# Another order of instructions for chunks 2 to 5 of an attention and feed-forward kernel

## The chip, the cores and the metric

The kernel runs on one core of one Trainium2 chip, in one launch. The metric is the device time of one execution in microseconds (us), the median over runs.

## What is computed

The first part is masked attention over 8 batches of 8 heads, 576 positions, 64 numbers a head. The first four heads of a batch look at the last 32 positions (local), the other four at every 32nd position before (strided). The second part is a feed-forward layer on the 4608 rows of 512 numbers that the heads give together, all in 32-bit floats:

```python
scores = scale * np.matmul(q, k.transpose(0, 1, 3, 2))
mask_local = (rel >= 0) & (rel < stride)
mask_strided = (rel >= 0) & (pos[None, :] % stride == pos[:, None] % stride)
...
attn = attn / (np.sum(attn, axis=-1, keepdims=True) + 1e-09)
x = np.ascontiguousarray(attn_out.transpose(0, 2, 1, 3)).reshape(B, S, H * D)
...
xn = (x - mu) / np.sqrt(var + 1e-06) * g_ln
ch = np.maximum(xn @ w_ch1, 0.0) @ w_ch2
return (x + ch).astype(np.float32)
```

w_ch1 is 512 x 2048, w_ch2 is 2048 x 512.

## The kernel before

**Chunks.** The 4608 rows are cut into nine chunks of 512 rows. Chunks 0 to 7 are the first 512 rows of each batch, chunk 8 the 64 rows left of each. A matrix product in full precision is three matmuls of TensorE: every operand is held as a high part (ScalarE rounds it) and a low part (the rest, by DVE or GpSimd), and high x high, high x low and low x high are added up in PSUM, where TensorE writes.

**Chunks 2 to 5** stand in `pair(c, p)` (L1317), with p from 0 to 7 for each chunk c, 32 calls. One call computes two of the 16 blocks of 128 columns of the first layer for all 512 rows, as a 2 x 2 block product by seven products in place of eight (Winograd's form). A product (`product2`, L1290, matmuls at L1299) is six matmuls 128 x 256. The weights' whole blocks a11, a12, a22 lie in SBUF, the four sums s1 to s4 of blocks are computed once in chunk 1 (`w_sums`, L802 on), kept in DRAM (`sd`) and brought back as needed: `stage_w(n)` (L1231) is a transfer sw<-sd issued by SyncE (SP), `split_w(n)` (L1236) makes high parts on ScalarE (L1240) and low parts on GpSimd (L1241). A call uses block n (s2 and one more sum) and n+1.

Products go to PSUM areas: x1 = a11 b11 with a12 b21 added later, x2 = s2 t2 with s3 t3 added, x3 = s1 t1 with s4 b22 added, x4 = a22 t4. Sums of these give four quarters: ScalarE copies x1 to p1 (L1331), DVE adds (`add2`, L1304) into u2, u3 and p1, and `quarter` (L1306) takes the relu's high part on ScalarE (L1309) and its low part on DVE (L1310). Each quarter puts two groups in a queue. A group (`group`, L889, matmuls at L902) is three matmuls 128 x 512 that add to an area po of the second layer; `run_groups(k)` issues k of the queue between products. After the last of 16 groups of an area `finish` (L874) takes it out (L876, DVE) and stores it (L879). Two areas po share one tile of two PSUM banks. Other areas: ps_h and ps_b one bank each, ps_m two.

**Attention beside it.** Heads are worked on in 32 twos (`Pair`s) that the generator `pieces` (L1071) hands out step by step, one `next(gen)` after each product. One step, `m_piece` (L687), is the block on TensorE: scores of the next two heads and outputs of these two (L452, L521), into ps_m (`m`) and the bank `n`. Behind it stand on DVE the mask (L480), the row maximum (L493) and the division of the outputs (`v_divide`, L571), on GpSimd the subtraction (L498), on ScalarE the exponential (L504). Others store the outputs (`v_store`, L584 to L589, SP), load them back in another shape (`x_raw`, L600, four transfers by ScalarE) and transpose them (`x_blocks`, L615, DVE), transpose q and k (`t_piece`, L427, DVE), load q and k (`load_qk`, L363, eight transfers by SP), v (`load_v`, L401 to L408) and x for the closing (`x_load`, L732 and L734). `half_c` (L1213) hands out the steps of statistics and x loads.

**What sets the order.** Each engine runs its instructions strictly in the order of the code, and the semaphores between them follow from the tiles. Transfers of SP and ScalarE are issued in those engines' order too. The x loads, the staged blocks and other input tiles share one pool of seven buffers. In `pair` the areas ps_h and ps_b change roles when a block has used one. Chunk 0 is set by a table; chunks 1 and 6 (`plain`, L1244) run the first layer in whole blocks of 512 columns, with attention beside; chunks 7 and 8 go through a loop with seven products of 512 columns (L1432) behind them.

## Time and profile before

| | us |
|---|---|
| median of the runs | 1019.4 (1016.4 and 1022.4) |
| the profiled execution, its own time | 1022.6 |
| its span | 1020.7 |
| TensorE (PE) busy | 906.2 (89%) |
| VectorE (DVE) busy | 567.0 (56%) |
| ScalarE (ACT) busy | 284.1 (28%) |
| GpSimd (POOL) busy | 350.9 (34%) |

Times in the trace count from the span's start. Matmuls are pipelined and their ends modelled, so the shares say how full an engine is, and not whether it is the limit. A wait is put down to the engine whose semaphore came last. PEclk is the mean clock that TensorE was granted as a share of full speed.

### The profile page before, as it was taken

To read this page: it belongs to the slowest core of one execution; us is meant where nothing else is said; L and a number is where in the kernel's file an instruction comes from. 1 tells how busy PE (TensorE), PEld (TensorE's weight loads), DVE (VectorE), ACT (ScalarE), POOL (GpSimd) and SP (SyncE) were. 2 spreads that over 40 slices of the span, in tenths; PEclk is the share of its full clock that TensorE was granted. 3 is DMA by queue.
4 is the path that set the end of the run, shared out by engine and by line. 5 is a ranking of instruction groups with operands and counts; after the bars stand their busy time and mean duration, and the time that the engine had idled before them with its cause. 6 is when DMAs were issued, how large, how long until landed. Compare 5 with 4: busy or idle time off the path is not lost. (4 is left out here: it accounts for less than half of the span.)

```text
span 1020.7 us, 20720 instructions
## 1 busy us (share of the span) xinstructions
PE 906.2 (89%) x7981; PEld 746.7 (73%) x7981; DVE 567.0 (56%) x1171; ACT 284.1 (28%) x590; POOL 350.9 (34%) x420
## 2 busy tenths in 40 slices
PE   7899989989688889889888888887879999999997
PEld 6688868777577767777677677666758787888776
DVE  5899943645655666565745565455345543333343
ACT  4786511111322232223222232222111122112121
POOL 5686725662424252324324252223100201112000
PEclk9999999999899999999899998999899999999999
DMA  9899646888576657756575576765566415332021
GB/s 191 220 261 295 145 94 152 199 205 185 148 165 139 128 132 194 155 132 135 152 164 125 119 161 172 152 151 128 120 183 116 95 42 186 103 104 72 8 76 42
DMA packets 382698, 146.64 MB, mean 144 GB/s; under 512 B 297732, under 2 KB 360072, under 8 KB 382600
## 3 DMA queue, kind: packets, MB, share of 16 engines
q1 hardware_dynamic: 305544, 131.23, 51.4%
q10 hardware_dynamic: 77056, 14.10, 7.8%
q8 instruction: 63, 1.03, 0.4%
q14 instruction: 35, 0.29, 0.1%
HBM read 104.56 MB, written 40.70 MB: 142 GB/s over the span
## 5 line engine op out<-in xcount | busy, mean ns | idle before, releaser
L902 PE MATMUL po<-w,hq 128*128 128x512 f32 x768 | 232.4, 417 | 22.9 <-ACT hq L1309 14.7
L902 PE MATMUL po<-w,hh 128*128 128x512 f32 x640 | 202.3, 398 | 7.4 <-DVE x L876 7.4
L902 PEld LDWEIGHTS po<-w,hq 128*128 128x128 f32 x768 | 136.0, 201 | 42.8 <-ACT hq L1309 16.5
L902 PEld LDWEIGHTS po<-w,hh 128*128 128x128 f32 x640 | 118.9, 190 | 35.2 <-DVE x L876 10.8
L902 PE MATMUL po<-w,hl 128*128 128x512 f32 x320 | 125.8, 393 | 0.0
L1299 PE MATMUL x<-xh_a,w 128*128 128x256 f32 x256 | 65.0, 314 | 32.0 <-ACT p L1331 25.6
L498 POOL TENSOR_TENSOR sm<-sm,mx 128x640 f32<-128x640 f32 (+1 forms) x31 | 39.4, 1270 | 143.9 <-DVE mx L493 128.7
L1299 PE MATMUL x<-xh_b,w 128*128 128x256 f32 x384 | 84.5, 283 | 1.9 <-DVE p L1304 1.8
L1299 PEld LDWEIGHTS x<-xh_a,w 128*128 128x128 f32 x256 | 48.7, 210 | 47.0 <-ACT p L1331 35.0
L870 DVE SCALAR_TENSOR_TENSOR hl<-ph,hh 128x512 fp32r<-128x512 f32 x48 | 32.9, 686 | 79.1 <-ACT hh L865 79.1
L1241 POOL TENSOR_TENSOR xh_a<-sw,xh_a 128x256 fp32r<-128x256 f32 x32 | 24.0, 749 | 149.4 <-ACT xh_a L1240 144.1
L744 POOL TENSOR_TENSOR rs<-rs,mhalf 128x1 f32<-128x1 f32 x36 | 20.4, 566 | 150.3 <-DVE rs L743 150.3
L1299 PEld LDWEIGHTS x<-xh_b,w 128*128 128x128 f32 x384 | 65.4, 188 | 8.0 <-DVE p L1304 2.6
L902 PEld LDWEIGHTS po<-w,hl 128*128 128x128 f32 x320 | 60.6, 189 | 13.0
L1241 POOL TENSOR_TENSOR w<-sw,w 128x256 fp32r<-128x256 f32 x64 | 47.2, 760 | 52.9 <-ACT w L1240 52.9
L865 ACT ACTIVATE hh<-ph 128x512 fp32r<-128x512 f32 x48 | 28.5, 595 | 131.1 <-PE ph L860 105.8
L1310 DVE SCALAR_TENSOR_TENSOR hq<-u,hq 128x256 fp32r<-128x256 f32 x64 | 30.8, 482 | 53.4 <-ACT hq L1309 53.4
L1304 DVE TENSOR_TENSOR u<-x,p 128x256 f32<-128x256 f32 x64 | 26.8, 419 | 53.9 <-ACT p L1331 36.0
L504 ACT ACTIVATE sm<-sm 128x648 f32<-128x648 f32 (+1 forms) x32 | 23.7, 741 | 109.9 <-POOL sm L498 105.0
L1299 PE MATMUL x<-xh_a 128*128 128x256 f32 x128 | 31.2, 306 | 26.1 <-DVE xo L571 13.3
L1299 PE MATMUL x<-xl_b,w 128*128 128x256 f32 x192 | 53.8, 280 | 0.0
L853 PE MATMUL ph<-xh,w 128*128 128x512 f32 x124 | 51.1, 412 | 2.5 <-DVE hl L870 2.5
(228 smaller groups left out, 1887.1 us busy)
## 6 DMA issues: line engine op xcount, KB each, us to landing
s<-in_moe_w_ch_dram SPq DMA_DIRECT2D x32, 512.0 KB
sw<-sd SPq DMA_DIRECT2D x64, 256.0 KB
out_dram<-x SPq DMA_DIRECT2D x32, 256.0 KB
raw<-in_q_dram SPq DMA_DIRECT2D x108, 72.0 KB
raw<-in_k_dram SPq DMA_DIRECT2D x108, 72.0 KB
wd<-w SPq DMA_DIRECT2D x24, 256.0 KB
ringa<-wd SPq DMA_DIRECT2D x24, 256.0 KB
xds<-xo SPq DMA_DIRECT2D x32, 162.0 KB
```

The costliest lines, as they stand in the source:

```text
L498: eng.tensor_tensor(out=sm, in0=sm, in1=mx[:, :, 0:nt].unsqueeze(3).broadcast_to([P, 2, nt, sm.shape[3]]), op=ALU.subtract)
L504: nc.scalar.activation(out=self.smv, in_=self.smv, func=AF.Exp, scale=SCALE)
L744: nc.gpsimd.tensor_tensor(out=rs, in0=rs, in1=mhalf, op=ALU.pow)
L853: nc.tensor.matmul(ph, w1h[:, cc], x[:, cc, :], start=(new and n == 0 and i == 0), stop=False)
L865: nc.scalar.activation(out=hh, in_=ph, func=AF.Relu)
L870: nc.vector.scalar_tensor_tensor(out=hl, in0=ph, scalar=0.0, in1=hh.bitcast(F32), op0=ALU.max, op1=ALU.subtract)
L902: nc.tensor.matmul(po[c, i], hx, w, start=(n_po[c, i] == 0 and n == 0), stop=(n_po[c, i] == NFC - 1 and n == 2))
L1241: nc.gpsimd.tensor_tensor(out=w[:, 1], in0=t[:, k], in1=w[:, 0].bitcast(F32), op=ALU.subtract)
L1299: nc.tensor.matmul(ps, wx, xx[:, j], start=(start and j == 0 and i == 0), stop=(j == 1 and i == 2), skip_group_check=not start)
L1304: nc.vector.tensor_tensor(out=out, in0=ps, in1=x, op=ALU.add)
L1310: nc.vector.scalar_tensor_tensor(out=hl, in0=src, scalar=0.0, in1=hh.bitcast(F32), op0=ALU.max, op1=ALU.subtract)
```

## The change

In `pair` the products come in the order a11, s2, s1, a12, s3, a22, s4 (before: a11, s2, a12, s3, s1, a22, s4), with four PSUM areas: x1 and later x4 in ps_h, x2 in ps_b, x3 in ps_m, which the attention block uses only at the start of an even pair. The block stands at a fixed place, ahead of the first product of each even p, and directly in front of it. The low parts of quarters (now a class `Quarter`) come one addition later, that of the last quarter in the next call; two groups run at the call's end. The exponential and its subtraction stand behind the copy of x1 and the split of block n+1; the split of n+2 stands ahead of the loads of x by ScalarE and of the relu q22. Loads and transposes of attention have fixed places. `finish` runs for the two areas of a po tile together. Around it: the sums in another order and on other engines, their store in three transfers, chunk 1 leaving seven groups instead of five, the last attention blocks in chunk 6, s1 before a12 in the loop of chunk 8.

The core of the diff (the function `pair` whole, then the small parts):

```diff
-    def quarter(c, f, i0, src):
-        t = hp_.tile([P, CH], F32R, tag=("hh", "hl")[i0 // 2], name=f"hq{c}_{f}_{i0}")
-        hh, hl = t[:, 0:HC], t[:, HC:CH]
-        nc.scalar.activation(out=hh, in_=src, func=AF.Relu)
-        nc.vector.scalar_tensor_tensor(
-            out=hl, in0=src, scalar=0.0, in1=hh.bitcast(F32), op0=ALU.max, op1=ALU.subtract)
-        add_groups(c, f, i0, (hh, hl))
-
-    def l1_bank(i, name):
-        return pools[i].tile([P, CH], F32, tag="h", name=name)[:, 0:HC]
+    class Quarter:
+
+        def __init__(self, c, f, i0, src):
+            self.key, self.src = (c, f, i0), src
+            t = hp_.tile([P, CH], F32R, tag=("hh", "hl")[i0 // 2], name=f"hq{c}_{f}_{i0}")
+            self.h = t[:, 0:HC], t[:, HC:CH]
+            nc.scalar.activation(out=self.h[0], in_=src, func=AF.Relu)
+
+        def low(self):
+            nc.vector.scalar_tensor_tensor(
+                out=self.h[1], in0=self.src, scalar=0.0, in1=self.h[0].bitcast(F32), op0=ALU.max,
+                op1=ALU.subtract)
+            add_groups(*self.key, self.h)
+
+    late = []
+
+    def late_low():
+        if late:
+            late.pop().low()
 
     def pair(c, p):
-        last = p == NFC // 2 - 1
+        even = p % 2 == 0
+        last, more = p == NFC // 2 - 1, c < wide - 2
         n = NFC * (c - 2) + 2 * p
-        end = NFC * (wide - 3) - 2
-        nv = visits[0]
-        third[0] = pools[1]
-        next(gen, None)
-        if visits[0] == nv:
-            pools.reverse()
-            third[0] = pools[1]
-        half_c(c, 2 * p)
-        run_groups(1)
-        x1 = l1_bank(0, f"x1_{c}_{p}")
+        fetch = n < NFC * (wide - 3) - 2
+        i = NHP * (c + 1) + p // 2
+        now, nxt = pairs[i], pairs[i + 1]
+        if even:
+            ps = bank(f"m{i}"), ps_b.tile([P, CH], F32, tag="h", name=f"n{i}")
+            parts = nxt.s_blocks(ps)
+            av = now.v_blocks(ps)
+            nxt.s_mask(parts)
+            late_low()
+            now.v_divide(av)
+            now.v_store()
+            nxt.s_max()
+        else:
+            late_low()
+        x1 = ps_h.tile([P, CH], F32, tag="h", name=f"x1_{c}_{p}")[:, 0:HC]
         product2(p, "a11", "b11", x1)
         nc.scalar.copy(out=p1_t, in_=x1)
-        next(gen, None)
         split_w(n + 1)
+        if even:
+            nxt.s_sub()
+            nxt.s_exp()
+        else:
+            nxt.p_load(nc.scalar)
         run_groups(1)
-        x2 = l1_bank(1, f"x2_{c}_{p}")
+        x2 = ps_b.tile([P, CH], F32, tag="h", name=f"x2_{c}_{p}")[:, 0:HC]
         product2(p, "s2", "t2", x2)
         add2(u2_t, x2, p1_t)
-        next(gen, None)
-        if last and c < wide - 2:
+        if even:
+            pairs[i + 2].load_v()
+        else:
+            now.x_blocks()
+        half_c(c, 2 * p)
+        if fetch:
+            stage_w(n + 2)
+        if last and more:
             x_split("b11")
         run_groups(1)
+        x3 = bank(f"x3_{c}_{p}")[:, 0:HC]
+        product2(p, "s1", "t1", x3)
+        if not even:
+            pairs[i + 2].t_piece()
+        run_groups(1)
         product2(p, "a12", "b21", x1, False)
-        quarter(c, 2 * p, 0, x1)
-        next(gen, None)
-        if last and c < wide - 2:
+        q = Quarter(c, 2 * p, 0, x1)
+        q.low()
+        if fetch:
+            split_w(n + 2)
+        if even:
+            nxt.p_turned()
+        if last and more:
             x_split("t2")
-        if n < end:
-            stage_w(n + 2)
+            x_split("t1")
         run_groups(1)
         product2(p, "s3", "t3", x2, False)
         add2(u3_t, x2, p1_t)
-        if last and c < wide - 2:
-            x_split("b21")
-        run_groups(1)
-        next(gen, None)
-        half_c(c, 2 * p + 1)
-        x3 = l1_bank(0, f"x3_{c}_{p}")
-        product2(p, "s1", "t1", x3)
         add2(p1_t, x3, u3_t)
-        quarter(c, 2 * p + 1, 2, p1_t)
-        next(gen, None)
-        if n < end:
-            split_w(n + 2)
+        if even:
+            now.x_raw(nc.scalar)
+        q22 = Quarter(c, 2 * p + 1, 2, p1_t)
+        if not even and i + 3 < NP:
+            pairs[i + 3].load_qk()
+        if fetch:
+            stage_w(n + 3)
         if last:
             late_x(c, 0)
         run_groups(1)
-        x4 = l1_bank(1, f"x4_{c}_{p}")
+        x4 = ps_h.tile([P, CH], F32, tag="h", name=f"x4_{c}_{p}")[:, 0:HC]
         product2(p, "a22", "t4", x4)
+        if even:
+            nxt.v_sums()
         add2(u3_t, x4, u3_t)
-        quarter(c, 2 * p + 1, 0, u3_t)
-        next(gen, None)
-        if n < end:
-            stage_w(n + 3)
+        q21 = Quarter(c, 2 * p + 1, 0, u3_t)
+        q22.low()
+        half_c(c, 2 * p + 1)
         if last:
             late_x(c, 1)
         run_groups(1)
         product2(p, "s4", "b22", x3, False)
         add2(u2_t, x3, u2_t)
-        quarter(c, 2 * p, 2, u2_t)
-        next(gen, None)
+        late.append(Quarter(c, 2 * p, 2, u2_t))
+        q21.low()
         if last:
             late_x(c, 2)
             late_x(c, 3)
         if p in (1, 7):
             w_whole(2 * (c - 2) + int(p > 1))
-        run_groups(1)
+        run_groups(2)
```

```diff
-        if n_po[c, i] == NFC:
+        if n_po[c, i] == NFC and i % 2:
+            finish(c, i - 1)
             finish(c, i)
...
-    LO = dict(b11=nc.vector, t2=nc.gpsimd, b21=nc.vector, t3=nc.gpsimd, t1=nc.vector, t4=nc.gpsimd,
-              b22=nc.vector)
+    LO = dict(b11=nc.vector, t2=nc.gpsimd, t1=nc.vector, b21=nc.gpsimd, t3=nc.vector, t4=nc.gpsimd,
+              b22=nc.gpsimd)
...
-    SUMS = ("s2", "s3", "s1", "s4")
+    SUMS = ("s2", "s1", "s3", "s4")
...
-            short = i < 3 * NHP - 1 or i in (25, 27, 29)
+            short = i < 3 * NHP - 1 or i >= NP - NHP
...
+        elif c < wide - 1:
+            at, late = (4, 5, 8, 9), 2
...
-    plain(1, NT - 1)
+    plain(1, 1)
...
+    late_low()
     run_groups(len(groups))
...
+    gen = pieces(NP - NHP, NP)
     plain(wide - 1, NT)
...
+        product(p, "s1", "t1", x3)
         product(p, "a12", "b21", x1, False)
         ha = h_pair(A, 2 * p, x1)
```

**Two places in the order of instructions.** The first is ScalarE in chunk 3, call p = 2. A row is line, operation, what is written, what is read and the shape; hq is a quarter's high part, sm the scores, p1 the copy of x1, w1_13, w1_15 the split block n+1 (in the place of a weight tile), xh_a and xl_a the split block n+2. Before:

```order
L1309 ACTIVATE hq3_2_2_4903<-u2_2145 128x256
L504 ACTIVATE sm0_191<-sm0_191 128x2x6x54
L1331 COPY p1_2144<-x1_3_2_4992 128x256
L1240 ACTIVATE w1_13_1844<-sw21_4891 128x256
L1240 ACTIVATE w1_15_2016<-sw21_4891 128x256
L1309 ACTIVATE hq3_4_0_5028<-x1_3_2_4992 128x256
L600 DMA xraw4_0_5046<-xdl_201 32x16x32 x4
L1309 ACTIVATE hq3_5_2_5067<-p1_2144 128x256
L1240 ACTIVATE xh_a_2142<-sw22_5031 128x256
L1240 ACTIVATE xl_a_2143<-sw22_5031 128x256
```

Now:

```order
L1314 ACTIVATE hq3_2_2_4901<-u2_2145 128x256
L1348 COPY p1_2144<-x1_3_2_4986 128x256
L1244 ACTIVATE w1_13_1844<-sw21_4875 128x256
L1244 ACTIVATE w1_15_2016<-sw21_4875 128x256
L504 ACTIVATE sm0_191<-sm0_191 128x2x6x54
L1314 ACTIVATE hq3_4_0_5039<-x1_3_2_4986 128x256
L1244 ACTIVATE xh_a_2142<-sw22_5018 128x256
L1244 ACTIVATE xl_a_2143<-sw22_5018 128x256
L600 DMA xraw4_0_5062<-xdl_201 32x16x32 x4
L1314 ACTIVATE hq3_5_2_5067<-p1_2144 128x256
```

The exponential (L504) has moved behind the copy and the split of n+1, and the split of n+2 (the last two L1240 rows) ahead of the loads of x and of the relu hq3_5_2.

The second place is DVE in the same call, from the start of the call; m and n are the outputs of the attention block in PSUM, den the rows' sums, xo the divided outputs, mx the row maximum. Before:

```order
L1310 SCALAR_TENSOR_TENSOR hq3_2_2_4903<-u2_2145,hq3_2_2_4903 128x256
L480 TENSOR_TENSOR sm0_191<-m4_0_4912,mask_s_137 128x2x5x54
L480 TENSOR_TENSOR sm0_191<-n4_0_4913,mask_s_137 64x54
L480 TENSOR_TENSOR sm0_191<-m4_0_4912,mask_s_137 64x54
L571 TENSOR_TENSOR xo_195<-n4_0_4913,den1_198 128x4x64
L571 TENSOR_TENSOR xo_195<-n4_0_4913,den1_198 64x64
L493 TENSOR_REDUCE mx4_3_4977<-sm0_191 128x12
L571 TENSOR_TENSOR xo_195<-m4_0_4912,den1_198 128x3x64
L571 TENSOR_TENSOR xo_195<-m4_0_4912,den1_198 128x64
L571 TENSOR_TENSOR xo_195<-m4_0_4912,den1_198 64x64
L1304 TENSOR_TENSOR u2_2145<-x2_3_2_5011,p1_2144 128x256
```

Now:

```order
L480 TENSOR_TENSOR sm0_191<-m17_4913,mask_s_137 128x2x5x54
L480 TENSOR_TENSOR sm0_191<-n17_4914,mask_s_137 64x54
L480 TENSOR_TENSOR sm0_191<-m17_4913,mask_s_137 64x54
L1317 SCALAR_TENSOR_TENSOR hq3_2_2_4901<-u2_2145,hq3_2_2_4901 128x256
L571 TENSOR_TENSOR xo_195<-n17_4914,den1_198 128x4x64
L571 TENSOR_TENSOR xo_195<-n17_4914,den1_198 64x64
L571 TENSOR_TENSOR xo_195<-m17_4913,den1_198 128x3x64
L571 TENSOR_TENSOR xo_195<-m17_4913,den1_198 128x64
L571 TENSOR_TENSOR xo_195<-m17_4913,den1_198 64x64
L493 TENSOR_REDUCE mx4_3_4984<-sm0_191 128x12
L1306 TENSOR_TENSOR u2_2145<-x2_3_2_5003,p1_2144 128x256
```

The low part of the quarter before (first row of before) has moved behind the mask, and all five divisions ahead of the row maximum.

## Rows read from the trace of the kernel before

**Rows 1.** Windows, chunks 2 to 5: stretch, length, busy PE PEld DVE ACT POOL, PEclk, DMA share, GB/s
```profile
251.70:370.70 119.00, 98.66 (x993) 82.44 (x992) 69.38 (x164) 34.72 (x88) 47.38 (x58) 0.97 0.66 151
370.70:487.20 116.50, 100.99 (x995) 85.03 (x994) 70.50 (x162) 32.49 (x83) 41.55 (x52) 0.96 0.64 149
487.20:606.40 119.20, 101.09 (x999) 84.62 (x1000) 70.50 (x161) 32.38 (x83) 41.06 (x52) 0.96 0.64 145
606.40:752.80 146.40, 116.29 (x1129) 96.44 (x1129) 78.87 (x178) 32.09 (x82) 35.55 (x43) 0.90 0.61 141
```

**Rows 2.** Waits of PE, 251.7 to 752.8: us in total, times, longest us
```profile
PE x L1299 <- ACT p L1331: 25.6, 18, 3.7
PE x L1299 <- DVE u L1304: 18.8, 15, 4.4
PE po L902 <- ACT hq L1309: 14.7, 8, 2.6
PE x L1299 <- DVE xo L571: 13.3, 5, 6.3
PE po L902 <- DVE x L876: 8.6, 7, 4.4
```

**Rows 3.** Timeline of PE, chunks 3 and 5: start, us, instruction, [idle before <-releaser]
```profile
441.78 0.86 PE L902 MATMUL po<-w,hq 128*128 128x512 f32 x3
...
443.19 0.86 PE L902 MATMUL po<-w,hq 128*128 128x512 f32 x3
...
730.10 1.48 PE L902 MATMUL po<-w,hq 128*128 128x512 f32 x3
```

**Rows 4.** Timeline around the start of an even pair of chunk 3
```profile
461.18 0.80 PE L452 MATMUL m<-kt_s,qt_s 64*64 64x54 f32 x40
...
463.05 0.72 DVE L480 TENSOR_TENSOR sm<-m,mask_s 128x540 f32<-128x540 f32 x1 [0.40 <-PE m L521]
...
463.93 0.54 DVE L571 TENSOR_TENSOR xo<-n,den 128x256 f32<-128x256 f32 x2
...
466.60 0.74 ACT L504 ACTIVATE sm<-sm 128x648 f32<-128x648 f32 x1 [4.39 <-POOL sm L498]
...
467.65 0.39 PE L1299 MATMUL x<-xh_a,w 128*128 128x256 f32 x1 [0.93 <-ACT p L1331]
```

**Rows 5.** Timeline of DVE in an odd pair of chunk 3
```profile
449.69 1.25 DVE L427 STREAM_TRANSPOSE qt_s<-raw 128x576 f32<-128x576 f32 x1
...
453.10 0.69 DVE L739 BATCH_NORM_STATS2 st<-x 128x6 f32<-128x512 f32 x1
...
454.22 0.77 DVE L615 STREAM_TRANSPOSE staged<-xraw 128x256 f32<-128x256 f32 x2
```

**Rows 6.** Timeline of SP and ACT in even pairs p2, p6, p0: store, and split
```profile
290.24 0.36 SPq L584 DMA_DIRECT2D xdl<-xo  x1
...
301.63 0.42 ACT L1240 ACTIVATE xh_a<-sw 128x256 fp32r<-128x256 f32 x1 [1.79 <-DMA sw<-sd]
...
349.03 0.37 SPq L584 DMA_DIRECT2D xdl<-xo  x1
...
352.92 1.93 ACTq L600 DMA_DIRECT2D xraw<-xdl  x4
...
356.60 0.42 ACT L1240 ACTIVATE xh_a<-sw 128x256 fp32r<-128x256 f32 x1 [0.85 <-DMA sw<-sd]
...
378.39 0.73 SPq L589 DMA_DIRECT2D xds<-xo  x2
...
388.24 0.42 ACT L1240 ACTIVATE xh_a<-sw 128x256 fp32r<-128x256 f32 x1 [1.33 <-DMA sw<-sd]
```

**Rows 7.** Windows, between issue and landing of sw in p2 (columns of Rows 1)
```profile
295.90:301.60 5.70, 4.58 (x26) 3.45 (x24) 2.17 (x7) 0.42 (x1) 0.00 (x0) 1.00 1.01 175
```

**Rows 8.** The page's costliest groups: busy, mean ns of one, idle before, releaser
```profile
L902 PE MATMUL po<-w,hh 128*128 128x512 f32 x640 | 202.3, 398 | 7.4 <-DVE x L876 7.4
```

**Rows 9.** Timeline of ACT at the last calls of chunk 5
```profile
726.77 0.42 ACT L1240 ACTIVATE xh_a<-sw 128x256 fp32r<-128x256 f32 x1 [7.84 <-DMA sw<-sd]
```

## What I predict, and why

> **What bounds the kernel now.** I read the busy shares by stage first [rows 1]. The four rows are chunks 2 to 5, the only ones whose instruction order changes in full. They take 119.0, 116.5, 119.2 and 146.4 us, together 501 of a span of 1020.7. TensorE (PE) is the busiest engine in each of them and still idles 20.3, 15.5, 18.1 and 30.1 us (length less its busy time); VectorE (DVE) is at about 60%. So this stage is a chain across engines: TensorE is the bound only where nothing keeps it waiting. The second view is TensorE's list of waits in the same stretch [rows 2]. Five kinds make 81 us: 25.6 for the copy of the first product (18 times, up to 3.7), 18.8 for an addition into u, 14.7 for a relu, 13.3 for the division of the attention outputs (one of 6.3 opens chunk 2), 8.6 for the closing operation L876. The third view is the order of time. When nothing is late, a product of six matmuls and a group of three follow one another in 1.41 us from 441.78 to 443.19 [rows 3], so I count 0.71 for a product and 0.70 for a group. After a stall the granted clock sinks: the group at 730.10 takes 1.48 us for three matmuls against 0.86 at 441.78, the lower of the two levels (1.2 instead of 2.4 GHz), behind 4.4 us of waiting.
>
> Two calls of pair() (an even and an odd p) hold 14 products, 16 groups and one attention block of about 1.75 us (it begins at 461.18 in [rows 4], and the mask, which waits for its last matmul, at 463.05): 9.9 + 11.2 + 1.75, with 0.3 for seams, is 23.1 us without a wait. Four such periods would be 92.6 us a chunk. I measured 116.5 in chunk 3, so about 6 us of every period is waiting or low clock.
>
> **The copy wait goes.** The timeline shows its cause [rows 4]. The mask starts on DVE at 463.05; the row maximum, the subtraction on GpSimd (POOL) and the exponential follow one another, and the exponential starts on ScalarE (ACT) only at 466.60, having waited 4.39 us for GpSimd. The copy of the first product stands behind it, and TensorE's a12 product, which adds to that same bank, starts at 467.65. With the exponential behind the copy, and a second and a third product between a11 and a12, nothing is left of the 25.6 us as long as those two products are free to run: s2 needs the bank of the attention outputs, so it waits for the division.
>
> **A smaller wait takes its place.** DVE now does mask (0.88: 463.05 to 463.93), the late low part (0.43) and the first division (0.54) ahead of it; the mask starts 1.87 us behind the block's start, so s2 may start at 3.8 us of the pair and is due at 3.2 (block 1.8, product and group 1.4). I count 0.6 us per even pair. Below, it could be nothing if the divisions overlap as those at 463.93 do; above, 1.9, all three operations in a row.
>
> **The staged halves of the first layer's weights set the new period.** ScalarE is strict in its order. In the new order the split of staged block n+2 (L1240 before, L1244 now) stands ahead of the x transposes' four DMAs on ScalarE and ahead of relu q22, so all of these wait for the landing. The timeline of SP and ScalarE [rows 6] gives the landing as time from the even pair's store of the attention output (first SP row) to the split's start, which waits for the sw transfer: 9.85 us in p0 (378.39 to 388.24), 11.4 in p2 (290.24 to 301.63), 7.6 in p6 (349.03 to 356.60). p4 is strided as p0 is and gets 9.85. SP's queue between the two is changed little (loads of v, of x, then sw, with sw(n+2) behind the same loads), so I take these values. The new store is issued at 4.35 us of the pair: 3.8, then two divisions' outputs. The landing L lies then at 14.2, 15.8, 14.2 and 11.9 us for p = 0, 2, 4, 6.
>
> From L, by rows: the two high parts 0.75 on ScalarE, the four DMA issues 2.1 (1.93 at 352.92), relu 0.42, so L+3.3; the low part on DVE 0.43 and the addition u2 0.42, L+4.2; then in the odd pair relu and copy on ScalarE, 0.9; addition 0.42, L+5.5; two transposes of x 0.77 (454.22) [rows 5]; two transposes of q and k, 2.5 where strided (1.25 each, 449.69); low part 0.43: L+9.2. Only then is the bank free for a22. a22, a group, s4 and two groups take 3.5: the next even pair starts at L+12.7. Where DVE has the statistics too (453.10, 0.69, and two small ones, 1.0 in all) and a local head's transposes (1.5 in place of 2.5), the sum is about the same; the odd pair behind p4 has statistics and strided transposes, L+13.6; that behind p6, local and without statistics, L+12.0.
>
> Periods: p0 26.9, p2 28.5, p4 27.8, p6 23.9 (this one is at the floor: 23.1 and the 0.6 above). The chunk's end falls in p0: 1.5 us more for four closings on DVE. Together 108.6 us a chunk.
>
> **The closing in twos.** po tiles hold two areas, and the next chunk's first matmul into a tile waited for its partner's closing. Such waits are 8.6 us in these chunks [rows 2] and 7.4 in the plain chunks' groups [rows 8]. When both areas of a tile are closed together, behind the second one's last group, DVE has the other tile's groups to do it in: four groups or more (2.8 us) against two closings of 0.75 (their cover; without it 1.5 us a chunk, which I left in p0). I take 7.4 and 1.6 for the low clock behind it: 9.
>
> **What moves without a price.** Low parts one addition later: DVE has the same count, and a queue of five to seven groups covers it (3.5 to 4.9 us of work); without that cover each costs up to 2.6, the longest of the relu waits. The sums' other order, the split sd store in three transfers instead of two, GpSimd for two more low parts: all in chunks 0 and 1 and behind full TensorE work. Chunk 6 takes over one attention block of chunk 5: moved, 1.9 us. Chunk 8's swapped products: nothing, TensorE is full there.
>
> **The sum**, against the profiled execution of 1022.6 us. Chunk 2: the 6.3 us opening wait depends on the late x of chunk 1 and mostly stays (5 of it): 119.0 − 113.6 = 5.4. Chunk 3: 116.5 − 108.6 = 7.9. Chunk 4: 119.2 − 108.6 = 10.6. Chunk 5: 108.6, and 4.9 for seven queued groups at its end, and 2 allowed for its last weights: 115.5, so 30.9, less the block moved 1.9: 29.0. Together 52.9. Closings 9. Against it, 8 for the low clock behind the new waits (2 a chunk; a stall like that at 730.10 costs 0.6 us a group). 1022.6 − 52.9 − 9 + 8 = 968.7. The profiled execution lay 3.2 above the median of 1019.4, so 965.5, rounded 966.
>
> **A rule against the staging.** In p2, between the issue of sw and its landing, the DMA engines are busy at 1.01 [rows 7]. The transfer lies behind others there, whichever engine issued them. The Trainium skill says the same under "DMA: Bandwidth & Descriptors", section "Issuing engines are not separate DMA queues": transfers of all issuing engines share the 16 DMA engines, and a second issuing engine saves only issue time. By that rule, the trace agrees, and taking ScalarE's x transfers from ahead of sw to behind it does hasten sw, which gives rival 1.
>
> **Rivals.**
> 1. The staged blocks land early, because the four x transfers that stood ahead of them are now behind. Then L is 11.9 in every pair, as in p6 now. Periods 24.6, 24.6, 25.5 and 23.9 and the 1.5: 100.1, 8.5 us a chunk, 34 in all: 932. For it: [rows 7]. Against it: p6 also has no loads of x ahead of sw. Chance 0.15.
> 2. The landing is later: the queue on SP now meets the x loads, which are allowed to stand ahead of sw. Each us of L costs one in p0, p2 and p4, 12 us in all, 16 when p6 is past its slack. 2.2 us later everywhere is about 998. From there to 1040 all counts as within 2%. Chance 0.14.
> 3. Slower: ScalarE's head of the line. In chunk 5 a split waited 7.84 us for its staged block [rows 9], that block having stood behind eight loads of q and k on SP; TensorE then stood 4.4. If stage_w, now moved between the loads, has to wait for one of the seven buffers that x and the staged blocks share, all three (x issue, q22, the copy of the odd pair) wait with it. It decides from 4.7 us of L in each even pair: 965 + 75 = 1040; at 7.84 it would be about 1090. Against it: sw(n+2) now stands ahead of the loads of q and k. Chance 0.08.
>
> **Chances.** The forecast, 945 to 990, has 0.63. Faster by over 2% (about what a measurement of this kernel can tell from no change; below 999) takes the forecast and rival 1: 0.78. Within 2%: 0.14. Slower: 0.08. The range goes from just below rival 1 to past the middle of rival 2: 930 to 1015.
>
> **What would show it.** TensorE's wait for the copy is gone, and the copy starts right behind x1. ScalarE's splits of sw wait longer in all, above 37 us, and they end in q22's relu. TensorE waits for the division by some 0.6 us an even pair. No matmul of a second layer waits for L876. Each of chunks 2 to 4 takes about 109 us with p6 the shortest period. The forecast is wrong if landings differ from L by more than 2 us, or if DVE's queue in the odd pair, not the landing, holds TensorE.

## The result, and the profile after

The changed kernel takes 969.0 us (968.8 and 969.2) against 1019.4: a ratio of 0.951, 95% interval 0.939 to 0.963. The forecast was 966. Its profiled span is 967.0 us, 53.7 less than before, and this is where they went. The windows of the kernel after have the columns of [rows 1]; the six rows are chunk 1, chunks 2 to 5 and chunk 6:

```profile
146.40:251.30 104.90, 95.58 (x879) 77.77 (x881) 51.52 (x106) 14.77 (x25) 56.15 (x62) 0.95 0.73 175
251.30:367.50 116.20, 100.41 (x998) 85.20 (x998) 68.50 (x166) 35.70 (x88) 48.51 (x59) 0.94 0.68 152
367.50:473.80 106.30, 95.84 (x992) 81.62 (x992) 65.73 (x160) 32.63 (x83) 41.98 (x52) 1.00 0.70 164
473.80:582.70 108.90, 97.86 (x992) 82.81 (x992) 65.68 (x160) 32.89 (x83) 42.24 (x52) 0.98 0.69 160
582.70:692.80 110.10, 100.53 (x1014) 85.77 (x1015) 66.40 (x158) 31.76 (x81) 34.08 (x42) 1.00 0.73 172
692.80:792.10 99.30, 94.15 (x794) 76.83 (x793) 51.41 (x105) 20.05 (x34) 12.34 (x12) 0.97 0.51 120
```

Set against the trace before, cut at the same places of the program (chunk 5 of before from 606.4 to its last group at 751.8):

| stretch | before, us | after, us | difference | forecast |
|---|---|---|---|---|
| to the first block of chunk 2 | 251.7 | 251.3 | -0.4 | -4 |
| chunk 2 | 119.0 | 116.2 | -2.8 | -5.4 |
| chunk 3 | 116.5 | 106.3 | -10.2 | -7.9 |
| chunk 4 | 119.2 | 108.9 | -10.3 | -10.6 |
| chunk 5 | 145.4 | 110.1 | -35.3 | -30.9 |
| chunks 6 to 8 | 268.9 | 274.2 | +5.3 | -3 |
| low clock, counted apart | | | in the rows above | +8 |

The forecast's 9 us of closings are divided here as those waits lay in the trace before (some 3 of 7 us at the start of chunk 1, the rest in chunks 7 and 8), and the block that moved from chunk 5 stands at chunks 6 to 8 with its 1.9. The total was right within 3 us, the parts were not: the first, second and sixth row gave 14 us less than forecast, chunks 3 and 5 gave 7 more, and the 8 us for a lower clock were not paid.

The list of TensorE's waits from 251.3 to 692.8, in answer to [rows 2] (us in total, times, longest us):

```profile
PE x L1301 <- DVE hq L1317: 16.5, 11, 2.5
PE x L1301 <- DVE xo L571: 10.0, 15, 3.1
PE po L903 <- ACT hq L1314: 5.6, 9, 1.4
PE po L903 <- DVE x L877: 5.1, 3, 2.0
PE n L521 <- DMA pt<-pd: 2.6, 1, 2.6
PE m L452 <- DVE u L1306: 2.5, 3, 0.9
```

The five kinds of [rows 2] were 81 us; all kinds are now 46. TensorE's idle time in chunks 2 to 5 (length less its busy time) was 84 us [rows 1] and is 47. These 37 us are most of the 59 that the four chunks lost; in the other 21 or so TensorE is busy for less time, by the block that moved and by the clock. The 25.6 us for the copy are gone, and so is nearly all of the wait for additions into u. A wait for low parts (L1317) has come, the one with which the prediction ended the odd pair.

The forecast's chain can be read off one period (an even call with the odd one behind it; it has the even call's name), p2 of chunk 3. Its attention block starts at 394.03. q22 is the quarter that is made from p1, and its relu is the row hq<-p. SP, ScalarE, DVE and TensorE:

```profile
398.07 0.36 SPq L584 DMA_DIRECT2D xdl<-xo  x1
...
402.52 0.41 SPq L1238 DMA_DIRECT2D sw<-sd  x1
```
```profile
407.23 0.42 ACT L1244 ACTIVATE xh_a<-sw 128x256 fp32r<-128x256 f32 x1 [5.25 <-DMA sw<-sd]
...
407.63 1.88 ACTq L600 DMA_DIRECT2D xraw<-xdl  x3
409.56 0.42 ACT L1314 ACTIVATE hq<-p 128x256 fp32r<-128x256 f32 x1 [1.60 <-issue]
```
```profile
410.00 0.43 DVE L1317 SCALAR_TENSOR_TENSOR hq<-p,hq 128x256 fp32r<-128x256 f32 x1 [4.42 <-ACT hq L1314]
...
412.55 0.77 DVE L615 STREAM_TRANSPOSE staged<-xraw 128x256 f32<-128x256 f32 x2 [0.23 <-DMA xraw<-xdl]
413.24 0.65 DVE L739 BATCH_NORM_STATS2 st<-x 128x6 f32<-128x512 f32 x1
...
415.56 0.39 DVE L1317 SCALAR_TENSOR_TENSOR hq<-x,hq 128x256 fp32r<-128x256 f32 x1
```
```profile
416.01 0.39 PE L1301 MATMUL x<-xh_b,w 128*128 128x256 f32 x1 [0.72 <-DVE hq L1317]
```

ScalarE waits 5.25 us for the staged block, issues the x loads, waits 1.60 for that issue, and only then takes the relu q22. Behind it DVE does low part, transposes and statistics, and TensorE's product a22 has to wait until 416.01. From the store (398.07) to the split (407.23) are 9.16 us, where 11.4 were assumed. The same distance is 7.15 in p0 (372.50 to 379.65), 9.13 in p4 (424.27 to 433.40) and 6.90 in p6 (450.19 to 457.09), against 9.85, 9.85 and 7.6.

The four periods of chunk 3 as windows:

```profile
367.47:394.03 26.56, 23.87 (x248) 20.50 (x249) 18.38 (x40) 8.68 (x22) 9.70 (x11) 1.00 0.70 186
394.03:419.71 25.68, 23.89 (x249) 20.34 (x248) 15.48 (x41) 7.05 (x19) 11.07 (x15) 1.00 0.83 188
419.71:446.14 26.43, 24.30 (x249) 20.58 (x248) 15.89 (x42) 7.48 (x20) 8.11 (x12) 1.00 0.59 141
446.14:473.81 27.67, 23.80 (x250) 20.24 (x249) 16.03 (x38) 9.41 (x23) 13.10 (x15) 1.00 0.70 141
```

They were forecast at 28.4 (with the closings), 28.5, 27.8 and 23.9. With the landings measured here, L is 12.2, 13.2, 13.7 and 11.0 after the block's start, and the sums L+12.7 with 1.5, L+12.7, L+13.6 and L+12.0 (at least 23.9) give 26.4, 25.9, 27.3 and 23.9. The first three are right within 0.9 us, and in chunks 2 to 5 all eleven periods of p0, p2 and p4 (without the first of chunk 2) lie within 1.0 us of such sums. The fourth is 3.8 short: something was left out there.

### The profile page after: what moved, and what is told of

The parts are those of the page before. It is cut to its first block, busy times and chain, and to the rows that moved or that the text cites. A ratio compares the mean times of both kernels' runs of the same rounds, so it can differ in the third digit from the quotient of the medians.

```text
span 967.0 us, 20717 instructions
## 1 busy us (share of the span) xinstructions
PE 889.5 (92%) x7981; PEld 739.1 (76%) x7981; DVE 550.8 (57%) x1167; ACT 285.5 (30%) x590; POOL 353.6 (37%) x424
## 3 DMA queue, kind: packets, MB, share of 16 engines
q1 hardware_dynamic: 300424, 130.44, 53.7%
q8 instruction: 63, 1.03, 0.4%
## 5 line engine op out<-in xcount | busy, mean ns | idle before, releaser
L903 PE MATMUL po<-w,hq 128*128 128x512 f32 x768 | 215.1, 396 | 10.7 <-ACT hq L1314 5.6
L903 PEld LDWEIGHTS po<-w,hq 128*128 128x128 f32 x768 | 130.1, 190 | 28.5 <-ACT hq L1314 7.5
L1301 PE MATMUL x<-xh_b,w 128*128 128x256 f32 x512 | 114.3, 286 | 18.0 <-DVE hq L1317 16.5
L1301 PEld LDWEIGHTS x<-xh_b,w 128*128 128x128 f32 x512 | 88.1, 190 | 30.7 <-DVE hq L1317 22.0
L1301 PE MATMUL x<-xl_b,w 128*128 128x256 f32 x256 | 72.2, 282 | 0.0
L1245 POOL TENSOR_TENSOR xh_a<-sw,xh_a 128x256 fp32r<-128x256 f32 x32 | 23.6, 737 | 129.2 <-ACT xh_a L1244 118.0
L866 ACT ACTIVATE hh<-ph 128x512 fp32r<-128x512 f32 x48 | 28.5, 594 | 106.4 <-PE ph L861 87.6
L1301 PEld LDWEIGHTS x<-xl_b,w 128*128 128x128 f32 x256 | 48.7, 190 | 4.7
L504 ACT ACTIVATE sm<-sm 128x648 f32<-128x648 f32 (+1 forms) x32 | 23.8, 744 | 87.3 <-POOL sm L498 87.3
L1176 POOL TENSOR_TENSOR rings<-stage,rings 128x512 fp32r<-128x512 f32 x16 | 20.6, 1289 | 77.8 <-ACT rings L1175 77.8
L854 PE MATMUL ph<-xl,w 128*128 128x512 f32 x124 | 48.4, 391 | 0.0
L1317 DVE SCALAR_TENSOR_TENSOR hq<-p,hq 128x256 fp32r<-128x256 f32 x32 | 16.0, 500 | 54.0 <-ACT hq L1314 54.0
L1244 ACT ACTIVATE xh_a<-sw 128x256 fp32r<-128x256 f32 x32 | 13.4, 417 | 96.0 <-DMA sw<-sd 90.9
```

Source lines behind the costliest of these rows:

```text
L504: nc.scalar.activation(out=self.smv, in_=self.smv, func=AF.Exp, scale=SCALE)
L854: nc.tensor.matmul(ph, w1h[:, cc], x[:, cc, :], start=(new and n == 0 and i == 0), stop=False)
L866: nc.scalar.activation(out=hh, in_=ph, func=AF.Relu)
L903: nc.tensor.matmul(po[c, i], hx, w, start=(n_po[c, i] == 0 and n == 0), stop=(n_po[c, i] == NFC - 1 and n == 2))
L1176: nc.gpsimd.tensor_tensor(out=t[:, :, 1], in0=stage[n], in1=t[:, :, 0].bitcast(F32), op=ALU.subtract)
L1245: nc.gpsimd.tensor_tensor(out=w[:, 1], in0=t[:, k], in1=w[:, 0].bitcast(F32), op=ALU.subtract)
```

## The experiments

Each kernel was timed beside the kernel before on one chip, and the ratio is taken there. The chips differ, so kernels are compared by their ratios, and the changed kernel was timed in this way once more. One thousandth of the ratio is 1.03 us. The intervals of two kernels together leave some 4 us open in the last column, and 7 for all edits that paid.

| kernel | ratio to before | 95% interval | against the changed kernel |
|---|---|---|---|
| changed kernel, again | 0.949 | 0.946 to 0.952 | |
| closing not in twos | 0.970 | 0.967 to 0.972 | +21 us |
| exponential ahead of the copy | 0.944 | 0.942 to 0.947 | -5 us |
| split of n+2 behind the relu | 0.934 | 0.931 to 0.936 | -16 us |
| loads of x and pt by SP | 0.934 | 0.932 to 0.936 | -15 us |
| these two together | 0.931 | 0.928 to 0.933 | -19 us |
| staged block first on SP | 0.925 | 0.922 to 0.927 | -25 us |
| no splits in p7 | 0.937 | 0.933 to 0.940 | -13 us |
| sums of chunk 1 a step later | 0.944 | 0.939 to 0.948 | -5 us |
| old order and exponential ahead | 1.061 | 1.056 to 1.065 | +114 us |
| all edits that paid | 0.917 | 0.911 to 0.923 | -33 us |
| before, with closing in twos | 0.987 | 0.984 to 0.991 | (-13 us to before) |

**The landing.** If one us of the landing is one us of the period, an earlier transfer of the staged block must shorten the kernel by more than anything else. The edit moves one call:

```diff
+        if fetch:
+            stage_w(n + 2)
         if even:
             pairs[i + 2].load_v()
         else:
             now.x_blocks()
         half_c(c, 2 * p)
-        if fetch:
-            stage_w(n + 2)
```

> The changed kernel, with the transfer of staged block n+2 issued by SP ahead of the loads of v and x in place of behind them: 2 to 4 us earlier in the even pairs. Theory of the landing (one us of it is one us of the period in p0, p2 and p4): 2 us in 12 pairs and less in the p6 ones, 20 to 30 us less than the changed kernel, ratio to before 0.92 to 0.93. Rival, from the last runs (the price was ScalarE's row ahead of the relu, not the landing itself, and the loads of v and x merely come later): 0 to 10 us, 0.94 to 0.95.

It measured 0.925, 25 us less, the middle of what the theory of the landing said. Pair p4 of chunk 3 in this kernel, SP and ScalarE:

```profile
416.85 0.72 SPq L589 DMA_DIRECT2D xds<-xo  x2
417.62 0.53 SPq L1238 DMA_DIRECT2D sw<-sd  x1
```
```profile
422.23 0.42 ACT L1244 ACTIVATE xh_a<-sw 128x256 fp32r<-128x256 f32 x1 [1.68 <-DMA sw<-sd]
...
423.01 3.14 ACTq L600 DMA_DIRECT2D xraw<-xds  x3
426.20 0.42 ACT L1314 ACTIVATE hq<-p 128x256 fp32r<-128x256 f32 x1 [3.24 <-DMA xraw<-xds]
```

The split starts 5.38 us after the store, 9.13 in the changed kernel. The relu q22 follows the store by 9.35 us (11.2 there), since the x loads now hold ScalarE for 3.1 us; the view puts the relu's wait down to one of these loads. So 3.75 us of landing became 1.85 at the relu, and the period went from 26.43 to 24.44, by as much. In p0 a landing 2.2 us earlier gave 2.0 (26.56 to 24.55). In p2 of this chunk 4.4 us gave nothing (25.68 to 25.67), and in p6 2.1 us gave nothing either (27.67 to 27.71), for a reason of its own (below, the fourth period). In p2 the next wait on ScalarE has taken over: the odd call's split now waits for the other staged block. Behind it the pt loads hold ScalarE for 3.1 us, and TensorE waits:

```profile
404.21 0.42 ACT L1244 ACTIVATE w<-sw 128x256 fp32r<-128x256 f32 x1 [2.91 <-DMA sw<-sd]
```
```profile
408.74 0.38 PE L1301 MATMUL x<-xh_b,w 128*128 128x256 f32 x1 [1.74 <-DVE hq L1317]
```

Waits of ScalarE for that other block are 40.7 us in chunks 2 to 5 of this kernel, 8.2 in the changed kernel. One us of landing is at most one us of the period, then, and only down to the next wait. The theory counted 2 us a pair; the landings came 1.8 to 5.3 us earlier, some 50 us over chunks 2 to 5, and at most half of that reached the time. That the whole met the middle of the expectation is in part luck.

**ScalarE's row behind the landing** is the other half of the chain. Two kernels shorten it in different ways, one by giving the issue to SP, the other by putting relu q22 ahead of the split:

```diff
-            nxt.p_load(nc.scalar)
+            nxt.p_load(nc.sync)
...
-            now.x_raw(nc.scalar)
+            now.x_raw(nc.sync)
```

> The changed kernel, with the loads of x (even pairs) and of pt (odd pairs) issued by SP in place of ScalarE, at the same place of the code. Theory of the landing with ScalarE's row behind it: 2.1 us of issue ahead of the relu q22 and 1.8 ahead of the odd pair's relu go, about 2 us in each of 16 periods, less where another wait stands next: 940 to 952 us. Rival: the second wait (division, DVE's queue of the odd pair) holds the same end: over 963.

```diff
         q.low()
-        if fetch:
-            split_w(n + 2)
...
         q22 = Quarter(c, 2 * p + 1, 2, p1_t)
+        if fetch:
+            split_w(n + 2)
```

> The changed kernel, with the split of staged block n+2 again behind the x loads of ScalarE and the relu q22. If what counts behind the landing is ScalarE's row (split 0.75, four issues 2.1, relu 0.42, all ahead of the low part), then 2.5 us of it now lie ahead of the landing, and against it the staged block lands some 1 us later because x comes first: 1.5 us less in 12 to 16 pairs, 945 to 951 us. Rival: the x loads push the landing back by 2.5 us or more: 969 or slower, up to 985.

They measured 15 and 16 us less, below the 17 to 29 and 18 to 24 expected of them, but clear. With SP issuing, the relu stands right behind the split (ScalarE, pair p2 of chunk 3):

```profile
406.13 0.42 ACT L1244 ACTIVATE xh_a<-sw 128x256 fp32r<-128x256 f32 x1 [5.47 <-DMA sw<-sd]
406.45 0.40 ACT L1244 ACTIVATE xl_a<-sw 128x256 fp32r<-128x256 f32 x1
406.76 0.40 ACT L1314 ACTIVATE hq<-p 128x256 fp32r<-128x256 f32 x1
```

The landing is as late as it was (5.47 us of waiting), only what followed it is gone. If both took away the same wait, they should not add:

> The changed kernel with both of the edits that shortened it: loads of x and pt issued by SP, and the split of n+2 behind the relu q22. If ScalarE's row behind the landing was the whole of the price, both take away the same wait (the relu behind landing and issue) and the sum is little more than either: 953 to 958. Rival: they are two prices (issue 2.1 us, landing ahead of the relu), and their gains of 10 to 13 us each add: 943 to 949.

They don't: 19 us together, where 31 would be the sum. It is one chain, landing and ScalarE's row behind it, and undoing the split's new place helps: that part of the change costs 16 us as it stands.

**The fourth period.** In p7 the operands of the next chunk are split (`x_split`), and the prediction had counted nothing for them. The kernel leaves these splits out:

```diff
         if last and more:
-            x_split("b11")
...
-            x_split("t2")
-            x_split("t1")
...
         if c < wide - 2:
-            x_split(OPERANDS[3 + k])
+            if k == 2:
+                del staged_x['t4']
```

> The changed kernel without the splits of the next chunk's first operands (seven in each of the last pairs p7 of chunks 2 to 4), so chunks 3 to 5 compute with the operands of chunk 2. Theory: those splits, 1.2 us each on DVE and 0.6 on ScalarE, which waits for their sources, are why the fourth period of a chunk takes 27.7 to 29.4 us where 23.9 was predicted: it falls to 24 to 25.5 in chunks 2 to 4, 9 to 12 us less in all, ratio 0.937 to 0.941. Rival: these periods are long for the landing or for the loads of q and k: under 3 us less.

The whole is 13 us less, and the period falls where it should (window of the fourth period of chunk 2 in this kernel):

```profile
340.03:364.00 23.97, 23.53 (x249) 20.35 (x248) 13.77 (x35) 6.97 (x19) 10.03 (x13) 1.00 0.76 150
```

It was 27.9 in the changed kernel, and is 23.8 and 23.6 in chunks 3 and 4, against the forecast's 23.9. The rival, that these periods are long for the landing, is out also by the three kernels above that shorten the chain by one edit: their fourth periods in chunks 2 to 4 stay at 27.7 to 30.3. The changed kernel shows how the splits do it (pair p7 of chunk 3, ScalarE, then DVE):

```profile
464.58 0.63 ACT L788 ACTIVATE xh_a<-staged 128x512 fp32r<-128x512 f32 x1 [1.50 <-DVE staged L615]
```
```profile
465.24 1.17 DVE L789 TENSOR_TENSOR xl_a<-staged,xh_a 128x512 fp32r<-128x512 f32 x1 [1.58 <-ACT xh_a L788]
...
467.69 0.38 DVE L1317 SCALAR_TENSOR_TENSOR hq<-x,hq 128x256 fp32r<-128x256 f32 x1
```

DVE stands 1.58 us for ScalarE and then works 1.17, ahead of the transposes and of the low part (467.69) for which a22 waits.

**The closing in twos** by itself, undone in the changed kernel and done in the kernel before:

```diff
-        if n_po[c, i] == NFC and i % 2:
-            finish(c, i - 1)
-            finish(c, i)
+        if n_po[c, i] == NFC:
+            finish(c, i)
```

> The changed kernel, with one part undone: finish again runs for each area of the second layer by itself, directly behind its last group. Theory of the prediction: the waits for the closing come back at every change of chunk, 7.4 us in the plain chunks and some 3 in chunks 2 to 4 and what the lower clock adds: 9 us more than the changed kernel's 969, so 976 to 980. Rival: where the changed kernel waits at those places for something else (in chunk 1 for pt, at the start of a pair for a landing), the closings are hidden behind it: 969 to 972.

> The kernel before, with one part of the change alone: finish runs for both areas of a po tile together. Theory of the prediction: this takes away the waits for the closing, 8.6 us in chunks 2 to 5 and 7.4 in the plain chunks, and some low clock behind them, 15 to 20 us less than before, if nothing else waits at those places: 1000 to 1005. Rival, from the traces (chunk 1 of the changed kernel gave 6 us back in waits for pt): 5 to 9 us less.

In the kernel before it is worth 13 us, between the two expectations. In the changed kernel it is worth 21, over twice what was expected. TensorE's waits from 251.3 to 720 without it, the longest of them in TensorE's row, and what DVE did there:

```profile
PE po L903 <- DVE x L877: 18.7, 10, 3.8
```
```profile
501.85 1.78 PE L903 MATMUL po<-w,hq 128*128 128x512 f32 x6 [3.81 <-DVE x L877]
```
```profile
500.71 0.43 DVE L1316 SCALAR_TENSOR_TENSOR hq<-p,hq 128x256 fp32r<-128x256 f32 x1 [2.54 <-ACT hq L1313]
501.05 0.74 DVE L877 SCALAR_TENSOR_TENSOR x<-po,rs,x 128x512 f32<-128x512 f32 x1
```

The closing stands on DVE behind the low part of q22, and that waited 2.54 us for ScalarE, whose relu waits for the landing. In the kernel before, TensorE's wait for a closing at this place was 0.94 us, once in each of chunks 3 to 5. So the new order alone would have made the closings dearer, since they queue on DVE behind the late low part; in twos they are off that way but for 5.1 us in three places of the changed kernel, of up to 2.0 us:

```profile
491.91 0.92 PE L903 MATMUL po<-w,hq 128*128 128x512 f32 x3 [2.04 <-DVE x L877]
```

Over the whole kernel TensorE waits 25.6 us for closings without the twos and 5.1 with them; the difference of 20.5 us agrees with the 21 measured. In the kernel before these waits were 15.6 us, and none is left of them with the twos, for 13 measured.

**The copy wait.** Which part of the change took away the 25.6 us?

```diff
             nxt.s_max()
+            nxt.s_sub()
+            nxt.s_exp()
...
-        if even:
-            nxt.s_sub()
-            nxt.s_exp()
```

> The changed kernel, with subtraction and exponential again ahead of the copy of x1 (right behind the row maximum). Theory of the landing: the even pair waits for the staged block anyway, and the copy, some 4 us later on ScalarE, first delays a12 by about 1.3 us, which the later wait for the landing gives back: 0 to 6 us over 969. Rival, the theory by which the copy was the cost: 1.3 us in each of 16 even pairs stay, 21 us more, about 990.

The wait comes back, but small (TensorE's waits from 250.8 to 690 in this kernel):

```profile
PE x L1301 <- ACT p L1350: 7.9, 15, 0.6
```

and the kernel is no slower: 0.944, 5 us less than the changed kernel, with intervals that touch, so whether it is faster stays open. The 0.5 us in each even pair are hidden before the landing. Of moving the exponential alone, nothing can be measured. The other half, the order of products, was to be tested with it:

> The changed kernel with the products in the old order (s1 behind s3, so one product between a11 and a12 in place of two; x3 stays in its own area) and the exponential again ahead of the copy. Theory of the prediction: TensorE waits for the copy again, 1.4 us or more in every even pair above what the exponential alone did (0.5 us each), 20 to 26 us: 994 to 1000, ratio 0.97 to 0.975. Rival: the wait for the landing stands in the same pair and takes up the delay: 0 to 8 us, ratio 0.949 to 0.957.

This kernel says nothing on that by its time, 114 us more than the changed kernel. In it the product s1 came behind the split of block n+2, which overwrites the place in which s1's weights lie; so it took the next pair's sum in place of its own, and TensorE waited for the landing inside every even pair (its waits from 250 to 800):

```profile
PE x L1301 <- ACT xl_a L1244: 42.0, 23, 4.2
PE x L1301 <- ACT p L1350: 30.9, 16, 2.0
PE x L1301 <- POOL xl_a L1245: 25.4, 30, 2.6
```

One thing can be read: the copy wait is there 16 times, about 1.93 us each, where it is 0.53 with two products between a11 and a12. The difference, 1.4 us, is a product and a group (1.41 [rows 3]). That the order of products is what covers the copy is seen in the waits, not measured in time. The run also shows that the new order goes with the early split: s1 ahead of a12 is what makes its place free.

**Chunk 1.** The closings at the end of chunk 0 went as forecast: from the first attention block of chunk 1 (146.42) to the second are 17.4 us, before 23.6. But the next period grew from 19.8 to 24.8, and chunk 1 as a whole gained 1.4 us. SP and TensorE in the changed kernel:

```profile
156.72 0.39 SPq L814 DMA_DIRECT2D sd<-f  x1
...
161.15 2.43 SPq L628 DMA_DIRECT2D pd<-sm  x4
163.90 3.34 SPq L642 DMA_DIRECT2D pt<-pd  x4
```
```profile
167.91 0.36 PE L521 MATMUL n<-v_s,pt 54*64 54x64 f32 x1 [3.14 <-DMA pt<-pd]
```

SP issues nothing from the block's start until the first sums are ready at 156.7; the stores and loads of the scores (pd and pt, which the attention block reads) stand behind. The change had begun the sums one step earlier. The experiment puts them back:

```diff
-    SUMS_AT = 0, 1, 3, 4, 6, 7, 9, 10
+    SUMS_AT = 1, 2, 4, 5, 7, 8, 9, 10
```

> The changed kernel, with the sums of chunk 1 begun at steps 1, 2, 4, 5, 7, 8, 9, 10 as before, in place of 0, 1, 3, 4, 6, 7, 9, 10. Theory: in chunk 1 SP stands at 156.7 for the first store of sums, and pd and pt, which the attention block then waits for (9.3 us in that chunk), are queued behind it; a step later the store stands behind them and 3 to 5 us of waits go, some of them given back later: 964 to 968. Rival: the transfers as a whole hold chunk 1 (DMA share 0.8 to 0.9), no gain: 968 to 973.

Chunk 1, from block to block, takes 99.7 us here (147.1 to 246.8) against 106.3 in the changed kernel on the same chip (147.6 to 253.9), 6.6 less; TensorE's waits for pt in it are 3.9 us, once. So the head of SP's line, not the transfers as a whole, held chunk 1. Over the whole kernel the gain is 5 us, with intervals that overlap, so how much of it lasts to the end stays open.

> The changed kernel as it is, so that the experiments have it beside them on one chip. Every theory expects the 969 us measured, give or take what chips differ by: a ratio of 0.945 to 0.951.

The repeated changed kernel lay at 0.949, where it was 0.951 on the first chip.

**A faster version.** All of what paid together: staged block first on SP, loads of x and pt by SP, split behind the relu, sums a step later, and the p7 splits spread behind q22, q21 and the last quarter:

> The changed kernel with what the runs so far showed to pay, together: the staged block n+2 issued first on SP, loads of x and pt issued by SP, split of n+2 behind the relu q22, the sums of chunk 1 begun a step later, and the splits of the next chunk's operands in p7 spread over its end, behind q22, q21 and the last quarter. Theory: all shorten the same way from a store to the next even pair, so they don't add, but the periods can come near the 23.1 to 23.9 of a pair without waits: 24.5 in each of 16, some 40 us less than the changed kernel in chunks 2 to 5, ratio to before 0.905 to 0.918. Rival: the two open pairs of waits (division in the even pair, transposes of DVE in the odd one) hold at 25: little below the staged block alone, 0.919 to 0.926.

It takes 940.7 us, 0.917 (0.911 to 0.923): faster than both kernels, 33 us less than the changed one (23 from the nearest ends of the two intervals, 0.923 and 0.946). Against the staged block first alone (0.925) the 8 us more are not clear of noise. Its chunks 3 and 4 take 104 to 105 us (block starts at 354.00, 457.81 and 562.95), 26 us a period: not the 24.5 that the theory hoped for, and above the rival's 25. Spreading the splits of p7 moved their price and did not take it away. The fourth period of a chunk and the first of the next take together 53.1, 54.0 and 54.1 us here, and 52.6, 53.9 and 53.9 with the staged block first alone. The largest wait left is the division's, 2.3 to 3.4 us in the first pair of each chunk and 0.4 in the others (TensorE's waits from 240 to 670 in this kernel, first and third):

```profile
PE x L1301 <- DVE xo L571: 15.0, 16, 3.4
...
PE x L1301 <- POOL w L1245: 2.9, 8, 0.6
```

## Why the prediction was right, point by point

- **What bounds the stage: right.** The chain store, landing, split, x issue, relu q22, low part, DVE's odd pair, a22 is in the trace of after step by step, and moving its first link (25 us) or its middle (15 and 16, not adding) showed its price. The formulas L+12.7 and L+13.6 held within 1.0 us at the landings of the changed kernel. With the staged block first, p2 should have come to the floor of 23.9 and stayed at 25.7, so they hold near these landings and no further. ScalarE's waits for staged blocks grew as forecast: the first split's from 37 us to 91 in chunks 2 to 5.
- **The landings: 0.7 to 2.7 us too long in chunk 3.** By the prediction's own sign, a landing over 2 us from L, this term failed: p2 landed 2.6 us before its L and p0 2.0. The times were taken from [rows 6] with the x loads ahead of the staged block on ScalarE; the change put these behind. That is rival 1's mechanism, and in chunk 3 the periods of p0, p2 and p4 came 1.8, 2.8 and 1.4 us under the forecast, where that rival had 2.3, 3.9 and 2.3: nearer to the rival. Of the 2.7 us in p0, 1.0 is SP's queue, of which the prediction had said that it changes little: sw is issued 3.8 us after the store in place of 4.8, where two stores of results stood ahead of it. About as much is the rival's mechanism: the split starts 3.3 us after SP's issue of sw, and 4.3 in the kernel with the split behind the relu, where the x loads are ahead again (5.0 in the kernel before). The rest is open. This mechanism agrees with the rule cited there, "DMA: Bandwidth & Descriptors" of the Trainium skill, that transfers of all issuing engines share the same DMA engines. But where that section calls the issue time usually small relative to the DMA itself, here the four x loads of p2 are issued from 407.29 to 409.51 and have landed at 412.55, so issue is 2.2 of 5.3 us. And what counts is who stands behind it: up to 2.4 us of ScalarE, and the loads of x and pt issued by SP made the kernel 15 us shorter.
- **The fourth period: the step that failed.** It was forecast at its floor, 23.9, as the shortest of the four, and came to 27.7, the longest. The missing term is the splits of p7, some 13 us in all. The floor itself was right, as the kernel without them shows. With the landings' error it cancels: 106.3 against 108.6 in chunk 3.
- **The copy wait: gone, as forecast, but its cause was told half.** Putting the exponential behind the copy brings nothing by itself that could be measured; two products between a11 and a12 leave 0.5 us of it, which the landing hides. What the order of products is worth in time, no run shows.
- **The smaller wait: there, and smaller.** For the division TensorE waits 15 times, eleven of them 0.35 to 0.39 us and three about 1 us, in the first pairs of chunks 3 to 5; 0.6 was forecast. One of 3.1 us opens chunk 2, where 5 of 6.3 were expected to stay.
- **The closings: forecast at 9 us outside chunks 2 to 5, where the waits went and the time did not.** The 6.2 us at the start of chunk 1 were given back to pt, as the sums had been put ahead of it on SP; in the kernel before, where they were not, closing in twos leaves chunk 1 at 98.4 us (145.0 to 243.4) in place of 106.3. Chunk 6 has one attention block more and a new wait for pt of 5.15 us, which ends at 717.47, and the lower clock from 716.4 to 723.2; why that transfer is late there was not tried. Inside the pairs the closing in twos is worth more than was counted, because the new order makes single closings late. That no matmul would wait for L876 did not come true: 5.1 us are left.
- **The clock: wrong sign.** 8 us were added for new waits. Length times (1 less PEclk), what the upper level would save at most, was 27.6 us in chunks 2 to 5 before (14.6 of it in chunk 5) and is 9.2 after. The waits left mostly did not take the clock from its upper level of 2.4 GHz: it was granted in full through chunks 3 and 5. In chunk 2 the lower level stands from 255.6 to 269.3, over the waits at its opening, 2.65 for pt and 3.06 for the division; in chunk 4 it stands once, for 3.4 us. The gain of chunk 5 above its forecast, 4.4 us, fits this; that it is the clock's alone was not tested.

So the total was near by compensation, which is luck and not foresight. In chunk 3 alone three periods were 6.0 us under the forecast and the fourth 3.8 over; over the whole kernel, earlier landings and the clock stand against the p7 splits and the gains that chunks 1 and 6 gave back.

## What to carry to other kernels

A wait that looks like one instruction's price is often a place in a row: before moving it, ask what the engine that stands in order has ahead of it next, here a staged transfer and four DMA issues on ScalarE. Put what feeds the next period first in its queue, and give DMA issues to an engine that nobody waits for. A gain at one place counts only when the next wait behind it has been looked at: here 6 us at the closing went to a store at the head of SP's line, and splits moved out of a chunk's last period came back in the next chunk's first.

## What was not expected of the hardware

- **Issuing is not free.** The issue of loads kept ScalarE's next relu waiting 1.33 to 2.43 us (13 waits ended by issue, 21.8 us in all in chunks 2 to 5; twelve of them behind the four x loads). One such issue took 0.31 to 1.58 us there.
- **A row of issues can stand for other transfers.** In the kernel with the split behind the relu, the four x loads of p2 in chunk 3 take 5.64 us from 402.14, though each issue takes 0.31. The rest lies between them, and the view puts the wait behind them down to another transfer, a store of the scores (pd<-sm). Which rule makes an issue stand, no run shows. The kernel before has such rows too (7.47 us from 408.54), and the prediction's 2.1 us came from a row without them.

```profile
407.83 0.42 ACT L1314 ACTIVATE hq<-p 128x256 fp32r<-128x256 f32 x1 [5.44 <-DMA pd<-sm]
```

- **The clock stayed up through some short waits, and not through others of the same length.** Chunk 3 of the changed kernel has thirteen waits of up to 1.8 us and a granted clock of 1.00, and at 362.27 a wait of 2.54 left it there. But in chunk 4 a wait of 2.24 had the lower level of 1.2 GHz around its end (0.51 from 576.4 to 579.8), which shows in the time of the same matmul behind it:

```profile
362.27 0.39 PE L1301 MATMUL x<-xh_b,w 128*128 128x256 f32 x1 [2.54 <-DVE hq L1317]
...
576.77 0.58 PE L1301 MATMUL x<-xh_b,w 128*128 128x256 f32 x1 [2.24 <-DVE hq L1317]
```

When the changed kernel was run again, its chunk 3 had the lower level too, for 3.4 us around a wait of 1.96 that ended at 388.42. So the length of a wait alone does not tell. In the kernel before, the lower level went with waits such as the 4.4 us behind which the group at 730.10 stands [rows 3].
